# A gated mix of attention and a state-space filter: TensorE's queue per group of scores, and zero matmuls sized to a set activity

## The chip, the cores and the metric

The kernel runs on one core of one Trainium2 chip. The metric is the device time of one execution in microseconds (us), as the median of several runs. The engines are TensorE (PE in the profile, with its weight loads as PEld), VectorE (DVE), ScalarE (ACT), GpSimd (POOL) and SyncE (SP, whose queue issues nearly all DMAs). Each engine works through its own queue strictly in the order in which the program wrote it.

## The reference, cut to what matters

```python
x = A_x                                            # 1 x 2048 x 512, bf16
g = sigmoid((x * gate_w).sum(-1, keepdims=True))
# a: attention, 32 heads of 16 channels, no mask
q, k, v = split_heads(x @ wqkv)
a = merge_heads(softmax(q @ k.T * 16 ** -0.5) @ v) @ wo
# b: per channel d a convolution of x over time with a kernel of 128 complex modes
dt   = exp(log_dt)
K    = einsum("dn,dnl,dn->dl", C, exp(dt * A * l), dt * B).real
b    = causal_conv(x, K) + x * Dskip
out  = g * a + (1 - g) * b
```

The attention part has 32 heads of 2048 x 2048 scores, and each score goes through an exponential.

## The kernel before, in words

**Slots and groups.** The scores are cut into 2048 *slots* of 128 keys x 512 queries of one head. Four slots (four heads of one half of a 128-channel strip) make a *quad*, 16 quads a *block* (512 queries, all keys), 32 blocks the whole. Independently of quads, three slots in a row make a *group*: there are 683 groups. For group g, TensorE writes three score matmuls into a PSUM tile of three banks, `SC[g % 2]` (`qk`, line 662), ScalarE takes the exponential of all three at once, 128 x 1536, into a ring of 15 slots in SBUF, `ET` (`ex`, line 673, L675). The values are accumulated per quad by four matmuls into the PSUM bank `OA` (`pv`, line 678); each of them takes four slots, so there are three value quads in four groups. After the 16th quad of a block, VectorE transposes `OA` out (`norm_a`, L689), and the next block may use the bank.

**Background.** Everything else is cut into small segments, written as Python generators ("threads") that yield an engine, a cost and a priority: the projections of queries, keys and values (`projs`), the gate (`gate`), the parameters, bases and tables of the state-space part on VectorE (`params`, `base`, `table`), its convolution kernels (`kstage`, tile `Kst`), its chunk states (`sstage`: `Qt` x `X2` into the bank `MB`, evicted to `Sst` by VectorE, L986 and L988), a scan over 32 chunks on VectorE (`scan`, L1037 to L1053, tiles `G`, `s2`, `s3`), its outputs (`ystage`: `Tt` x `X2` and `Py` x `SG` into `MB`, evicted to `Yst`, L1118) and the output projection (`outs`, `Wo`). All of these share the one PSUM bank `MB`, taken with a lock.

**What sets the order.** The program is written out by a planner when it is built. The planner keeps a modelled clock for every engine (`p.tm`), adds a written-in cost for every instruction (`c=`), and a latency (`lat=`) before another engine may see its result. For each group it records the exponential, then the score matmuls of the next group, and then calls `fill`, which picks segments whose modelled start is early enough: a PE segment is taken if it would end by `pe_until`, 0.35 us after the modelled end of ScalarE's queue. A value quad is one of these segments, with a priority that excuses it from the test of its end.

**Zero matmuls.** After `fill`, the planner may add matmuls of a tile of zeros, `wm`, that accumulate zeros into `OA` and change nothing. Each instruction on PE has a count `a`, its columns weighted by the share of the 128 x 128 array that it uses: 512 for a matmul of 512 columns on the whole array, 128 for a score or a value matmul of 512 columns (a quarter of the rows, or of the columns). `p.act` sums these counts over a group.

```python
        sch.fill(t, t + .35)
        lack = min(lack, 1536) + FILL - p.act
        b = sch.now
        while lack > 256 and b is not None and p.tm["PE"] < t + .2:
            mm(OA ..., wm ..., wm ...)          # 512 columns
            lack -= 512
        p.act = 0
```

`FILL` is 1400. `lack` is carried from group to group; it is cut off above 1536 and not cut off below. `b` is the block whose accumulation is open in `OA`. All PE instructions are recorded through one helper, `mm`, so that they all stand under line L551 in the profile, and are told apart by their tiles: `SC<-Qm,KT` are scores, `OA<-ET,VE` values, `OA<-wm` zeros, `MB<-...` background. At the end of the build `place` lays the SBUF tiles out, tiles whose lifetimes do not meet on the same bytes, with waits for what lay there before.

Of the kernel before, what the change touches and what calls it, by code (L numbers as in the profile page):

```python
# [10 lines left out]
ALU = mybir.AluOpType  # L11

P = 128
S = 2048
D = 512
# [8 lines left out]
FILL = 1400  # L24
# [31 lines left out]
class Prog:  # L56
# [61 lines left out]
    def ready(self, a):  # L118
        eng, R, W = a[1][0], a[1][2], a[1][3]
        t = 0.0  # L120
        for acc, wr in ((R, False), (W, True)):
            for b, sl, *tag in acc:
                st = b.st.get(sl)
                if not wr and (st is None or not st[0] or (tag and b.tags.get(sl) != tag[0])):
                    return None
                if st is None:
                    continue
                for d in (st[0], st[1]) if wr else (st[0],):
                    for s, i in d.items():
                        if s != "PE" or eng != "PE":  # L130
                            t = max(t, self.fin[(s, i)] + (0 if s == eng else .08))
        return t
# [28 lines left out]
    def op(self, eng, fn, R=(), W=(), c=.1, lat=.05, a=0):  # L161
        if self.cap is not None:
            self.cap.append((self.op, (eng, fn, R, W), dict(c=c, lat=lat, a=a)))
            return
        self.act += a
        self.log.append((self.op, self.q, (eng, fn, R, W)))
        deps = self._deps(eng, R, W)
        i = self.cnt[eng]
        at = self.tm[eng]
        for s, k in deps.items():  # L170
            at = max(at, self.fin[(s, k)] + (0 if s == eng else .08))
        self.tm[eng] = at + c
        self.fin[(eng, i)] = at + c + lat
        self.cnt[eng] += 1
        self._record(eng, fn, deps, eng, i, R, W)
        return at + c + lat
# [58 lines left out]
class Sched:  # L235


    def __init__(self, prog):
        self.p = prog
        self.thr = []  # L240
        self.flag = set()
        self.lock = {}
        self.now = None
        self.n = 0

# [79 lines left out]
    def fill(self, until, pe_until):  # L325
        while True:
            best = None
            for t in self.thr:
                e = self.est(t)
                if e is None:  # L330
                    continue
                if t.eng == "PE":
                    if e + t.cost > pe_until and t.up > 0 or e > pe_until:
                        continue
                elif e > until:
                    continue
                now = self.p.tm[t.eng]
                k = (max(e, now + .3) if e > now + .02 else now, t.up, t.n)
                if best is None or k < best[0]:
                    best = (k, t)  # L340
            if best is None:
                return
            self.issue(best[1])
# [22 lines left out]
def declare(nc, es):  # L366
# [75 lines left out]
    sb("X2", 4 * 32 * 64)  # L442
# [19 lines left out]
def place(nc, bufs):  # L462
# [20 lines left out]
    for k in range(400):  # L483
# [7 lines left out]
        if best is None or top < best[0]:  # L491
            best = (top, order)
    assert best[0] <= end, (best[0] - end, live(sbs))
# [38 lines left out]
def dv(n, r=1):  # L532
    return .1 + n * 1.045e-3 / r


def record(nc, p, B, ins):
# [10 lines left out]
    MM, QUAD, TRI = .23, .34, .33  # L547
# [85 lines left out]
    def proj_ev(kind, idx, c, bank):  # L633
# [3 lines left out]
           [(o, ky)], c=.65)  # L637

    def vproj_mm(pi, kq, i, q4):
        kt = 4 * kq + i  # L640
        mm(lambda: MB(128 * i, [[1, 128]]), lambda: xT(q4 * S + 128 * kt, [[1, 128]]), lambda: B["Wv"](q4 * D + 128 * pi, [[1, 128]]),
           [xk(kq, q4), (B["Wv"], 0)], [(MB, 0, ('p', "V", pi, kq))], q4 == 0, q4 == 3, c=.08, a=128)

    def vproj_ev(pi, kq):
        op("DVE", lambda v: v.tensor_copy(VE((pi * 16 + 4 * kq) * VW, [[VW, 4], [17, 8], [1, 16]]),
                                          MB(0, [[128, 4], [16, 8], [1, 16]])),
           [(MB, 0, ('p', "V", pi, kq))], [(VE, (pi, 4 * kq + i)) for i in range(4)], c=.68)

    def mk_qm(b):
        qc, pi, w = b // 8, (b % 8) // 2, b % 2  # L650
        op("DVE", lambda v: v.tensor_scalar(Qm(512 * (b % 2), [[1, 512]]), B[f"Q{qc}"](512 * pi, [[1, 512]]),  # L651
                                            msk(w, [[1, 1]]), None, ALU.mult), [(B[f"Q{qc}"], pi), (msk, 0)], [(Qm, b % 2, b)], c=.32)
# [20 lines left out]
    def ex(g):  # L673
        sc, e, n = SC[g % 2], (3 * g) % NS, len(slots(g))
        op("ACT", lambda a: a.activation(ET(512 * e, [[1, 512 * n]]), sc(0, [[1, 512 * n]]), AF.Exp, scale=DH ** -0.5),  # L675
           [(sc, i, g) for i in range(n)], [(ET, s % NS, s) for s in slots(g)], c=.063 + .4267 * n, lat=.1)
# [11 lines left out]
    def norm_a(b):  # L688
        op("DVE", lambda v: v.transpose(OT(0, [[1, 512]]), OA(0, [[1, 512]])), [(OA, 0, b)], [(OT, 0, b)], c=.72)  # L689

    def norm_b(b):
# [3 lines left out]
                                            Rz(16 * w, [[1, 16], [0, 16]]), ALU.mult), [(OT, 0, b), (Rz, w)], [(ON, w)], c=.4)  # L695

    def norm_c(b):
        qc, pi = b // 8, (b % 8) // 2
        op("DVE", lambda v: v.transpose(OnT[qc](pi * 512, [[1, 512]]), ON(0, [[1, 512]])), [(ON, 0), (ON, 1)],
           [(OnT[qc], pi)], c=.7)  # L700
# [153 lines left out]
    def base(qr, eng):  # L854
# [4 lines left out]
        for l, n in ((0, "VV"), (1, "VL")):  # L859
            yield (eng, .38)  # L860
            op(eng, lambda v, l=l, n=n: v.tensor_copy(FP(l, [[e8, 2], [8, 128]]), B[n](d0, [[D, 2], [1, 128]])), key(n), [(FP, 0)], c=.38)
# [30 lines left out]
    def table():  # L892
# [3 lines left out]
        for pb in range(NBLK // 2):  # L896
# [9 lines left out]
            for i in range(2):  # L906
                yield ("DVE", .4)
                op("DVE", lambda v, i=i, b0=b0, B16=B16: v.tensor_copy(PT(i * PTN, [[CB * T, 2], [T, CB], [1, 16]]),
                                                                     B16(b0 + i * CB * 16, [[2048, 2], [16, CB], [1, 16]])), bk, [W[i]], c=.38)
# [21 lines left out]
    X2 = B["X2"]  # L931
# [37 lines left out]
    def sstage(blk):  # L969
        yield ("AFTER", f"ub{blk // 4}")  # L970
        q0, qr, bl = (blk % 2) * PTN, blk // 4, blk % 4
        for bank in range(4):
# [3 lines left out]
            for pp in range(2):  # L976
                yield ("PE", .29)
                for j in range(4):
                    k, par = 4 * bank + 2 * pp + j // 2, j % 2
                    mm(lambda pp=pp, j=j: MB(256 * pp, [[1, 256]], 32 * j, 32),  # L980
                       lambda k=k, par=par: X2(2048 * qr + 16 * bl + k, [[64, 32]], 64 * par, 64),
                       lambda k=k, par=par: Qt(q0 + 128 * k, [[16 * 128, 2], [1, 128]], 64 * par, 64),
                       [(Qt, (blk % 2, k // 8), blk), (Qt, (blk % 2, 2 + k // 8), blk), (X2, (qr, par))], [(MB, 0, ('S', blk, bank))], pos=(64 * par, 32 * j),
                       c=.29 if j == 0 else 0, a=32)
            yield ("DVE", .8, -1)
            op("DVE", lambda v, bank=bank: v.tensor_copy(Sst(512 * bank, [[256, 2], [1, 128]]), MB(0, [[256, 2], [1, 128]])),  # L986
               [(MB, 0, ('S', blk, bank))], [(Sst, bank, (blk, bank))], c=.37)
            op("DVE", lambda v, bank=bank: v.tensor_scalar(Sst(512 * bank + 128, [[256, 2], [1, 128]]), MB(128, [[256, 2], [1, 128]]),  # L988
                                                           -1.0, None, ALU.mult),
               [(MB, 0, ('S', blk, bank))], [(Sst, (bank, 1), (blk, bank))], c=.37)  # L990
# [32 lines left out]
    def scan():  # L1023
# [4 lines left out]
        def quarter(qr):  # L1028
# [4 lines left out]
            for c in range(NCH - 1):  # L1033
                so = 2 * SGH * (c + 1)
                if c == 0:
# [9 lines left out]
                yield (e, .38)  # L1045
                op(e, lambda v, so=so: v.tensor_tensor(s2(0, [[128, 2], [1, 128]]), s2(0, [[128, 2], [1, 128]]),  # L1046
                                                             sg(so, [[SGH, 2], [1, 128]]), ALU.add),
                   [(s2, 0)] + ks, [(s2, 0)], c=.38)
                yield (e, .38)
                op(e, lambda v: v.tensor_tensor(G(0, [[1, 256]]), s2(0, [[1, 256]]), s3(0, [[1, 256]]), ALU.add),  # L1050
                   [(s2, 0), (s3, 0)], [(G, 0)], c=.38)
# [38 lines left out]
    def ystage():  # L1090
        def unit(u):
# [8 lines left out]
            for q in range(4):  # L1100
                yield ("PE", .2)
                for j in range(4):
                    par, k = j % 2, 2 * q + j // 2
                    mm(lambda q=q, j=j: MB(64 * q, [[1, 64]], 32 * j, 32),
                       lambda k=k, par=par: X2(2048 * qr + 16 * bl + 8 * hf + k, [[64, 32]], 64 * par, 64),
                       lambda k=k, par=par: Tt(r * 512 + 64 * k, [[1, 64]], 64 * par, 64),
                       [(X2, (qr, par)), (Tt, (r, par, k // 4), u)], ky, True, False, pos=(64 * par, 32 * j), c=.2 if j == 0 else 0, a=8)
                yield ("PE", .35)
                for ri in range(2):
                    for j in range(4):  # L1110
# [5 lines left out]
                           pos=(0, 32 * j), c=.2 if j == 0 else 0, a=16)  # L1116
# [22 lines left out]
    def ublocks():  # L1139
        yield ("AFTER", "base1")  # L1140
        for qr in range(4):
            for par in range(2):
                yield ("SP", .5)
                dma("SP", lambda e, qr=qr, par=par: e.dma_start(X2(2048 * qr, [[64, 32], [1, 64]], 64 * par, 64),
                                                               B["xrd"].dram(64 * qr + 256 * par, [[32 * D, 64], [D, 32], [1, 64]])),
                    [(B["xrd"], 0)], [(X2, (qr, par))], c=.5, lat=5)
# [48 lines left out]
    def outs():  # L1195
# [3 lines left out]
        for lt in range(16):  # L1199
# [4 lines left out]
            for pi in range(3 if lt >= 12 else 4):  # L1204
# [6 lines left out]
               [(MB, 0, ('o', lt)), (Yl, ("c", lt))] + key("g"), W, c=.68)  # L1211
# [5 lines left out]
    def projs():  # L1217
# [5 lines left out]
        for kind, i, c in todo:  # L1223
            yield ("LOCK", "MB")
            for q4 in range(4):
                if kind == "V":
                    yield ("PE", .32)
# [71 lines left out]
    for q4 in range(4):  # L1299
        proj_mm("K", 0, 0, (SC[0], 0, 0), q4)  # L1300
    op("DVE", lambda v: v.tensor_scalar(Qm(0, [[1, 512]]), OA(0, [[1, 512]]), msk(0, [[1, 1]]), None, ALU.mult),
       [(OA, 0, ('p', "Q", 0, 0)), (msk, 0)], [(Qm, 0, 0)], c=.68)
# [23 lines left out]
    for g in range(NG):  # L1326
# [11 lines left out]
        sch.fill(t, t + .35)  # L1338
        lack = min(lack, 1536) + FILL - p.act
        b = sch.now  # L1340
        while lack > 256 and b is not None and p.tm["PE"] < t + .2:
            mm(lambda: OA(0, [[1, 512]]), lambda: wm(0, [[1, 128]]), lambda: wm(0, [[1, 512]]), [(wm, 0)], [(OA, 0, b)], False, False)
            lack -= 512
# [15 lines left out]
    for i in range(4):  # L1359
# [4 lines left out]
           [(b, sl, ('o', lt)), (fp, lt - 12)] + key("g"), [(fo, lt % 4, lt)], c=.68)  # L1364
# [35 lines left out]
```

## Time and profile before

| | |
|---|---|
| median of 3 runs | 1030.11 us (1026.2, 1030.11, 1030.48) |
| the profiled execution, span from first to last instruction | 1023.2 us |
| what the median has beyond that span | 6.9 us |
| ACT busy | 946.5 us (93%) |
| PE busy | 866.9 us (85%), 7076 matmuls |
| DVE busy | 611.4 us (60%) |
| mean clock granted to TensorE | 0.690 of full speed |
| exponentials | 683, 939.4 us busy together |
| zero matmuls in `OA` | 276 (nine of them before the first group), 123.5 us |

The profile gives no time of the profiled execution besides its span; what lies around the span is taken from the median. A busy PE in this profile is not a PE at its peak, since the ends of matmuls are modelled. The granted clock is listed in the profile as full or half speed over stretches of time; a mean such as 0.690 is a mix of these two. Durations of one instruction overlap with the next one's on the same engine, so that the pace is read from start to start or from busy time over count: an exponential of 128 x 1536 is listed as 1508 ns, and 109 of them in a row take 146.46 us, 1.344 us each.

The order of the background in time: projections until 152 us, tables and bases on VectorE, chunk states from 222 to 492 us, outputs of the state-space part from 460 to 708 us, output projection from 715 us on. From about 775 us to the last exponential at 1012.56 us there is little on TensorE besides scores, values and zeros.

### The profile page before, as it was taken

What the parts mean: (1) busy time and instruction counts of PE and PEld (TensorE: products, weight loads), DVE (VectorE), ACT (ScalarE), POOL (GpSimd) and SP (SyncE); (2) the same over time, 40 slices, a digit from 0 to 9 for tenths busy, and PEclk for the clock granted to TensorE, in tenths of its full rate; (3) what the DMA queues carried; (4) which work ended last, traced back from release to release, by engine and by line L of the source; (5) the groups of instructions that cost most, each with busy time, mean ns of one, the idle gap of its engine ahead of it and who ended that gap; (6) DMA issues with size and microseconds to landing.
All of it is one profiled execution on the core that took longest, in us unless ns stands there. A gap on an engine that the chain in (4) does not pass through costs nothing.

```text
span 1023.2 us, 17025 instructions
## 1 busy us (share of the span) xinstructions
PE 866.9 (85%) x7076; PEld 246.4 (24%) x7076; DVE 611.4 (60%) x1382; ACT 946.5 (93%) x693; POOL 11.9 (1%) x15
## 2 busy tenths in 40 slices
PE   7888788789889888889989899899887787787786
PEld 3332322112112222223323233233211111111111
DVE  4899999987678998878889988702310000000201
ACT  6999999999889999989999999999999899989985
POOL 4000000000000000000000000000000000000000
PEclk9999995555556887655565665755957766767757
DMA  8200005259997788696475725142100000000000
GB/s 180 83 2 1 2 1 83 103 119 202 232 240 176 170 186 208 187 176 165 108 145 145 168 75 148 40 124 48 42 11 11 1 1 1 1 1 1 1 1 21
DMA packets 228940, 92.21 MB, mean 90 GB/s; under 512 B 193408, under 2 KB 216576, under 8 KB 226816
## 3 DMA queue, kind: packets, MB, share of 16 engines
q1 hardware_dynamic: 227136, 90.22, 38.5%
q10 hardware_dynamic: 1728, 0.92, 0.4%
q8 instruction: 55, 0.90, 0.3%
q14 instruction: 21, 0.17, 0.0%
HBM read 27.92 MB, written 35.65 MB: 62 GB/s over the span
## 4 chain that ended last, share of the span: by engine, by line
ACT 51%; PE 41%; DVE 2%; SPq 2%; DMA 2%; issue 2%; ACTq 0%; DVEq 0%
ACT ET L675 51%; PE OA L551 19%; PE SC L551 14%; PE MB L551 9%; SPq L1017 1%; DMA Wq<-in_A_wqkv_dram 1%; DMA Qt<-gm_ptd 0%; SPq L937 0%; DVE Sst L986 0%; DMA Tt<-gm_kpd 0%; DVE Sst L988 0%; DVE OT L689 0%; DVE Kst L958 0%; SPq L994 0%; ACTq L555 0%
## 5 line engine op out<-in xcount | busy, mean ns | idle before, releaser
L675 ACT ACTIVATE ET<-SC 128x1536 bf16<-128x1536 f32 (+1 forms) x683 | 939.4, 1508 | 62.1 <-PE SC L551 55.7
L551 PE MATMUL OA<-ET,VE 128*32 128x512 bf16 x2048 | 268.6, 514 | 117.4 <-ACT ET L675 114.1
L551 PE MATMUL SC<-Qm,KT 32*128 32x512 bf16 x2048 | 353.2, 511 | 11.3 <-ACT ET L675 9.7
L551 PEld LDWEIGHTS SC<-Qm,KT 32*128 32x128 bf16 x2048 | 69.5, 95 | 275.9 <-issue 203.6
L551 PE MATMUL OA<-wm 128*128 128x512 bf16 x276 | 123.5, 573 | 1.2 <-DVE wm L604 1.2
L551 PEld LDWEIGHTS OA<-ET,VE 128*32 128x32 bf16 x2048 | 56.8, 100 | 268.9 <-ACT ET L675 242.0
L651 DVE TENSOR_SCALAR Qm<-Q,msk 128x512 bf16<-128x512 bf16 x31 | 10.6, 342 | 178.7 <-PE SC L551 178.7
L689 DVE STREAM_TRANSPOSE OT<-OA 128x512 f32<-128x512 f32 x32 | 22.9, 714 | 74.2 <-PE OA L551 74.1
L703 DVE TENSOR_TENSOR tt<-B,D 128x1024 bf16<-128x1024 bf16 x96 | 63.2, 683 | 0.3
L1050 DVE TENSOR_TENSOR G<-s,s 128x256 f32<-128x256 f32 x120 | 50.7, 422 | 3.4
L551 PE MATMUL MB<-Qt,X 64*32 64x256 bf16 x512 | 43.3, 392 | 8.8 <-issue 3.2
L1040 DVE TENSOR_TENSOR s<-G,MU 128x256 f32<-128x256 f32 x120 | 50.1, 417 | 0.1
L1046 DVE TENSOR_TENSOR s<-s,SG 128x256 f32<-128x256 f32 x120 | 50.1, 417 | 0.0
L1043 DVE TENSOR_TENSOR s<-G,MU 128x256 f32<-128x256 f32 x120 | 50.0, 417 | 0.0
L551 PE MATMUL MB<-Py,SG 128*32 128x64 bf16 x1024 | 44.1, 259 | 0.0
L1118 DVE CAST Yst<-MB 128x256 bf16<-128x256 f32 x32 | 13.5, 423 | 50.7 <-PE MB L551 50.5
L986 DVE CAST Sst<-MB 128x256 bf16<-128x256 f32 x64 | 27.0, 422 | 24.3 <-PE MB L551 23.8
L551 PEld LDWEIGHTS OA<-wm 128*128 128x128 bf16 x276 | 27.5, 119 | 57.4 <-issue 52.3
L1053 DVE CAST SG<-G 128x256 bf16<-128x256 f32 x120 | 34.9, 291 | 3.0
L551 PE MATMUL MB<-Tt,X 64*32 64x64 bf16 x512 | 35.7, 267 | 0.2 <-DMA Tt<-gm_kpd 0.2
L551 PEld LDWEIGHTS MB<-Py,SG 128*32 128x32 bf16 x1024 | 27.5, 150 | 34.9 <-issue 31.8
L703 DVE TENSOR_TENSOR ft<-FP,L 128x1024 f32<-128x1024 f32 (+1 forms) x32 | 33.8, 1079 | 0.0
(123 smaller groups left out, 470.2 us busy)
## 6 DMA issues: line engine op xcount, KB each, us to landing
gm_ptd<-PT SPq DMA_DIRECT2D x16, 1024.0 KB, 5.1
Py<-gm_ptd SPq DMA_DIRECT2D x32, 512.0 KB, 4.3
gm_sd<-Sst SPq DMA_DIRECT2D x64, 128.0 KB, 2.7
gm_kpd<-Kst SPq DMA_DIRECT2D x16, 256.0 KB, 4.3
Tt<-gm_kpd SPq DMA_DIRECT2D x128, 32.0 KB, 3.5
gm_xrd<-in_A_x_dram SPq DMA_DIRECT2D x1, 2048.0 KB, 12.1
X<-gm_xrd SPq DMA_DIRECT2D x8, 256.0 KB, 4.9
gm_ytd<-Yst SPq DMA_DIRECT2D x32, 64.0 KB, 4.0
```

The costliest lines, as they stand in the source:

```text
L551: op("PE", lambda t: t.matmul(out(), lhsT(), rhs(), start=start, stop=stop, skip_group_check=True, **kw), R, W, c=c, lat=.15, a=a)
L651: op("DVE", lambda v: v.tensor_scalar(Qm(512 * (b % 2), [[1, 512]]), B[f"Q{qc}"](512 * pi, [[1, 512]]), msk(w, [[1, 1]]), None, ALU.mult), ...
L675: op("ACT", lambda a: a.activation(ET(512 * e, [[1, 512 * n]]), sc(0, [[1, 512 * n]]), AF.Exp, scale=DH ** -0.5), [(sc, i, g) for i in ran ...
L689: op("DVE", lambda v: v.transpose(OT(0, [[1, 512]]), OA(0, [[1, 512]])), [(OA, 0, b)], [(OT, 0, b)], c=.72)
L703: op(eng, lambda v: v.tensor_tensor(o(), a(), b_(), f), R, W, c=c)
L986: op("DVE", lambda v, bank=bank: v.tensor_copy(Sst(512 * bank, [[256, 2], [1, 128]]), MB(0, [[256, 2], [1, 128]])), [(MB, 0, ('S', blk, ba ...
L1040: op(e, lambda v: v.tensor_tensor(s2(0, [[128, 2], [1, 128]]), G(0, [[128, 2], [1, 128]]), MU(d0, [[0, 2], [1, 128]]), ALU.mult), key("G", ...
L1043: op(e, lambda v: v.tensor_tensor(s3(0, [[128, 2], [1, 128]]), G(128, [[-128, 2], [1, 128]]), MU(D + d0, [[D, 2], [1, 128]]), ALU.mult), k ...
L1046: op(e, lambda v, so=so: v.tensor_tensor(s2(0, [[128, 2], [1, 128]]), s2(0, [[128, 2], [1, 128]]), sg(so, [[SGH, 2], [1, 128]]), ALU.add), ...
L1050: op(e, lambda v: v.tensor_tensor(G(0, [[1, 256]]), s2(0, [[1, 256]]), s3(0, [[1, 256]]), ALU.add), [(s2, 0), (s3, 0)], [(G, 0)], c=.38)
L1053: op(e, lambda v, so=so: v.tensor_copy(sg(so, [[SGH, 2], [1, 128]]), G(0, [[128, 2], [1, 128]])), key("G"), ks if c < NCH - 2 else [(sg, b ...
L1118: op("DVE", lambda v: v.tensor_copy(Yst(r2 * 256, [[1, 256]]), MB(0, [[1, 256]])), ky, [(Yst, r2, u)], c=.37)
```

## The change

It rewrites what the planner puts into TensorE's queue for each group, and the planner's costs.

1. **Order within a group.** A PE segment is no longer taken if its modelled start lies past the end of ScalarE's queue, value quads included. The value matmuls whose exponentials end with the present group are therefore written one group later; the order in the queue becomes scores of the next group, values that have ended, background, zeros.
2. **Size of the zeros.** The wanted count per group is `FILL`, now 1600, plus what the last group lacked, between -256 and 768. Background on PE is only taken if there is room left for the zeros that are still wanted (`room`). Zeros come in matmuls of 512 or of 256 columns, up to 0.3 us past ScalarE's modelled end. When `OA` is closed between two blocks, they go to `MB`, if no thread holds it.
3. **Pauses.** In the first 4 of every 14 groups the PE segments of threads with priority 2 or 5 (`sstage`, `ystage`, `gate`) are not taken, and the wanted count is at least 1792.
4. **The model's numbers.** Costs of VectorE and PE operations are written lower by a few hundredths of a microsecond, and the latencies between engines are changed.
5. **Tiles.** The tile `X2` becomes four tiles, and each quarter's two loads wait for its own `base` mark instead of all for `base1`. `place` tries up to 12,000 more layouts if the first 400 do not fit.

```diff
-FILL = 1400
+ZCOL = .213 / 512
+FILL = 1600
+OVER = .3
+REST = (14, 4, 1792)
+DLAG = .05
...
-                            t = max(t, self.fin[(s, i)] + (0 if s == eng else .08))
+                            t = max(t, self.fin[(s, i)] + (.03 if s == eng else DLAG if eng == 'PE' and s == 'DVE' else .05))
...
-    def op(self, eng, fn, R=(), W=(), c=.1, lat=.05, a=0):
+    def op(self, eng, fn, R=(), W=(), c=.1, lat=.085, a=0):
...
-    def fill(self, until, pe_until):
+    def fill(self, until, pe_until, want=0):
...
                 if t.eng == "PE":
-                    if e + t.cost > pe_until and t.up > 0 or e > pe_until:
+                    if self.rest and t.prio in (2, 5):
+                        continue
+                    own = sum(a[2].get("a", 0) for a in t.seg if isinstance(a, tuple))
+                    room = max(0, want - self.p.act - own) * ZCOL
+                    if e + t.cost + room > pe_until and t.up > 0 or e > min(until, pe_until):
                         continue
...
-    sb("X2", 4 * 32 * 64)
+    for k in range(4):
+        sb(f"X2{k}", 32 * 64)
...
+    k = 0
+    while best[0] > end and k < 12000:
...
 def dv(n, r=1):
-    return .1 + n * 1.045e-3 / r
+    return .07 + n / 960 / r
...
-    MM, QUAD, TRI = .23, .34, .33
+    MM, QUAD, TRI = .24, .33, .32
...
     def ublocks():
-        yield ("AFTER", "base1")
         for qr in range(4):
+            yield ("AFTER", f"base{min(qr + 1, 3)}")
...
         t = p.tm["ACT"]
-        sch.fill(t, t + .35)
-        lack = min(lack, 1536) + FILL - p.act
-        b = sch.now
-        while lack > 256 and b is not None and p.tm["PE"] < t + .2:
-            mm(lambda: OA(0, [[1, 512]]), lambda: wm(0, [[1, 128]]), lambda: wm(0, [[1, 512]]), [(wm, 0)], [(OA, 0, b)], False, False)
-            lack -= 512
+        want = FILL + min(max(lack, -256), 768)
+        sch.rest = g % REST[0] < REST[1]
+        if sch.rest:
+            want = max(want, REST[2])
+        sch.fill(t, t + OVER, want)
+        lack = want - p.act
+        p.act = 0
+        while lack >= 256 and p.tm["PE"] < t + OVER:
+            b = sch.now
+            if b is not None:
+                bank, W = OA, [(OA, 0, b)]
+            elif sch.lock.get("MB") is None:
+                bank, W = MB, [(MB, 0, "zero")]
+            else:
+                break
+            n = 512 if lack >= 512 else 256
+            mm(lambda bank=bank, n=n: bank(0, [[1, n]]), lambda: wm(0, [[1, 128]]), lambda n=n: wm(0, [[1, n]]), [(wm, 0)], W,
+               bank is MB, bank is MB, c=n * ZCOL, a=n)
+            lack -= n
         p.act = 0
```

The other edits of the diff are written-in costs of single operations (for example .65 to .62 for an eviction of 128 x 512, .29 to .22 for four matmuls of the chunk states).

## Prediction

> **What bounds the kernel now.** I read the page first: busy shares, the 40 slices, the costly groups.
>
> ```profile
> span 1023.2 us, 17025 instructions
> ...
> PE   7888788789889888889989899899887787787786
> ...
> ACT  6999999999889999989999999999999899989985
> ...
> PEclk9999995555556887655565665755957766767757
> ...
> L675 ACT ACTIVATE ET<-SC 128x1536 bf16<-128x1536 f32 (+1 forms) x683 | 939.4, 1508 | 62.1 <-PE SC L551 55.7
> ```
>
> ScalarE's 683 exponentials fill the span, and its idle time is spent waiting for scores. The clock row is full in the first six slices and a mix of full and half afterwards. Next, the chain that ended last, in order of time:
>
> ```profile
> 18.42 146.46 ACT ET L675 x109
> ...
> 809.76 1.82 PE OA L551 x4
> ```
>
> The first line is the pace when nothing disturbs it: 146.46 / 109 = 1.344 us a group. The second is typical of what interrupts it later: four matmuls into `OA` of 0.455 us each. Busy time and clock in stretches of 25 us (PE, PEld, DVE, ACT, POOL, then the clock):
>
> ```profile
> 125.00:150.00 25.00, 20.68 (x144) 5.41 (x142) 23.43 (x39) 25.00 (x20) 0.00 (x0) 1.00 0.00 1
> 175.00:200.00 25.00, 20.29 (x130) 3.80 (x126) 22.67 (x40) 24.51 (x19) 0.00 (x0) 0.50 0.38 124
> 600.00:625.00 25.00, 25.00 (x312) 9.21 (x308) 21.20 (x63) 23.48 (x18) 0.00 (x0) 0.50 0.52 128
> ```
>
> At full clock ACT is busy 25.00 of 25 us, and VectorE at 94% does not hurt it; at half clock ACT falls to 23.48. What sets the clock shows in two neighbouring stretches of 3.41 us, which is the length in which the trace lists it, first all engines, then zeros alone:
>
> ```profile
> 787.87:791.29 3.42, 1.91 (x21) 0.50 (x18) 1.40 (x3) 3.06 (x3) 0.00 (x0) 1.00 0.00 0
> 791.29:794.70 3.41, 3.41 (x18) 0.75 (x14) 0.00 (x0) 2.63 (x3) 0.00 (x0) 0.50 0.00 0
> ...
> 787.87:791.29 3.42, 0.00 (x0) 0.00 (x0) 0.00 (x0) 1.00 0.00 0
> 791.29:794.70 3.41, 1.89 (x4) 0.43 (x4) 0.00 (x0) 0.50 0.00 0
> ```
>
> Counted as the kernel counts (512 for a zero, 128 for a score or value matmul; weight loads do not straddle the edges), the first has 18 x 128 = 2304 and is followed by a half-clock stretch; the second has 10 x 128 + 4 x 512 = 3328 and is followed by a full one. I did this count for every 3.41-us stretch of the trace, spreading each matmul over its columns: above about 3000 the next stretch is full, below it half, with three exceptions in some 290. At 1.344 us a group a stretch holds 2.54 groups, so 1185 a group keeps the clock.
>
> Finally the durations, from TensorE's timeline around 803 us (full clock) and 809 us (half):
>
> ```profile
> 803.23 0.40 PE L551 MATMUL OA<-ET,VE 128*32 128x512 bf16 x4 [0.62 <-ACT ET L675]
> 803.56 0.39 PE L551 MATMUL SC<-Qm,KT 32*128 32x512 bf16 x3
> 803.89 1.04 PE L551 MATMUL OA<-wm 128*128 128x512 bf16 x4
> 804.86 0.39 PE L551 MATMUL SC<-Qm,KT 32*128 32x512 bf16 x3
> ...
> 808.60 0.62 PE L551 MATMUL OA<-ET,VE 128*32 128x512 bf16 x4 [0.62 <-ACT ET L675]
> 809.15 0.61 PE L551 MATMUL SC<-Qm,KT 32*128 32x512 bf16 x3
> 809.70 1.89 PE L551 MATMUL OA<-wm 128*128 128x512 bf16 x4
> 811.51 0.49 PE L551 MATMUL SC<-Qm,KT 32*128 32x512 bf16 x3
> ```
>
> From start to start: values 0.33 and 0.55, scores 0.33 and 0.55, four zeros 0.97 and 1.81. The zeros come four at a time in one group of four: only the group without a value quad passes the planner's test of PE's time. At half clock those 1.81 us delay the scores, and ACT idles 0.8 us.
>
> **The floor.** The first exponential starts at 14.54 us, the last at 1012.56 us; 682 steps of 1.344 are 916.4. So 1012.56 - 14.54 - 916.4 = 81.6 us is lost. Sorted by the clock at each step, 81.2 of it lies in the 401 groups at half clock (9.0 from 150 to 286 us, 13.9 to 450, 27.1 to 712, 31.2 to 1013), at full clock nothing. Without loss the span is 1023.2 - 81.6 = 941.6 us. Medians lie 6.9 us above the span; I add that.
>
> **The change, part by part.**
>
> *Zeros at 1600 a group, with the debt cut.* Ahead of the first group 33 matmuls count 512 each, 16,900; the 101 groups to 150 us count some 1664 each, 264 over `FILL`, which makes `lack` about -43,600. From 150 to 286 us the 94 groups count 913 each, so `lack` climbs by 487 a group, 45,800 together: no zero is written until 286 us, and the clock is 0.52 there. With the cut at -256 that goes. Scores and values count 768 a group, so 832 columns of zeros or background are added. At full clock a group takes PE 0.33 + 0.75 x 0.33 + 832 x 0.97 / 2048 = 0.97 us of 1.344: hidden behind ACT. 1600 x 2.54 = 4064 against 3000 keeps the clock. If that cover goes (half clock), the group takes 0.55 + 0.41 + 832 x 1.81 / 2048 = 1.70 us and costs 0.35 on the path, but counts 1600 x 3.41 / 1.70 = 3210 a stretch and so ends itself.
>
> *The same with background.* The bank `MB` keeps PE 110 us over the 286 groups from 286 to 712 us, 0.38 a group, worth some 130 in the count. At half clock: 0.55 + 0.41 + 0.38 + 702 x 1.81 / 2048 = 1.96 us, 0.62 lost a group, 1600 x 3.41 / 1.96 = 2780: below 3000, so this holds itself down. The pause is what ends it: 0.96 + 1024 x 1.81 / 2048 = 1.87 us and 1792 x 3.41 / 1.87 = 3270 a stretch; four such groups last 7.5 us, more than two stretches, so one lies whole inside. An episode is then some 5 groups at 0.62 and 3 of the pause at 0.52: 4.7 us.
>
> *What starts an episode.* After 25 us PE stalls for over 1 us, other than for ACT, three times before the tail: 2.52 us at 280.1 (chunk states wait for the load of `Qt`), 2.23 at 293.1 (the scan's first operation waits 4.95 us for `SG` on VectorE, an eviction stands behind it, `kstage` behind that), 1.25 at 447.0 (`Qt`). ACT loses 2.92, 2.47 and 1.25. The loads are unchanged, so I keep all three: 6.6 us. The two long ones leave too little in their stretch to keep the clock: 2 x 4.7 = 9.4 us.
>
> *Values one group later.* No instruction is added. The ring has 15 slots, five groups, and the exponential that reuses a slot comes four groups after the values now do: zero. If that cover went, ACT would wait one quad, 0.33 us.
>
> *Pauses.* They delay background by at most 14/10. From 222 to 712 us that is 196 us if PE set its pace; VectorE, busy 85% there, sets it. Even so the output projection, now from 715 us on, would end before the last group: zero.
>
> *Zeros into `MB`* wait for VectorE's last read of it, with the next scores behind them: at most 0.42 us (an eviction, row of `Sst`), once in each of 32 blocks, inside the 0.37 us that PE has free: zero, bound 13.
>
> *Cheaper VectorE in the model.* 1024 elements in bf16 (row of `tt`) go start to start in 0.60 us, 0.635 in the old model, 0.603 in the new. Taken at zero; background matmuls wait now 11.8 us for `Sst`, which I keep as the bound above, and as much below.
>
> *`X2` in four, other layout.* The same eight loads of 256 KB on SP's queue, 4.9 us each; the last two come later, past `base2` and `base3`, with `Qt` and `ptd` transfers behind them, and `sstage` needs the last only for its last quarter. Zero; a new wait from bytes shared otherwise is bounded by one stall like the one at 280 us, 2.5, to either side.
>
> Sum: 941.6 + 6.6 + 9.4 = 957.6 us of span, 964.5 of time. The bounds taken at zero (13, 12 and 2.5 upwards) stay for the range.
>
> **A rule against it.** From 784 to 822 us PE never idles more than 0.95 us between matmuls, and five of the eleven 3.41-us stretches are at half clock; from 600 to 625 us it is busy all 25 us at 0.50. The Trainium skill, TensorE: Matmul & The Clock Gate, "Why this matters for your kernels", asks for no idle gaps above about 3 us to keep the rate. By that rule zeros would fill no gap that matters and the third rival below would hold; the trace disagrees.
>
> **The rivals.**
>
> 1. *Half clock between pauses* in part of the state-space stretch: more stalls than three, each lifted only by the next pause. 60 more groups at 0.62 give 37 us: about 1002. For it: chunk states and outputs there run at 0.50 now. Against it: at full clock (327 to 341 us) chunk states cost nothing. 0.16.
> 2. *The pauses do not lift the clock*, because `OA` is closed or `MB` locked within them, or a kernel segment lies inside. Then the 330 groups from 222 to 708 us stay at half clock and the larger zeros sit on the path: 205 us, 941.6 + 6.6 + 205 + 6.9 = 1160. It turns slower than now from (81.6 - 6.6) / 0.62 = 121 such groups on. For it: 3270 is only 9% above the threshold; against: `OA` is closed in one group of 21. 0.09.
> 3. *The clock does not follow the count.* Then all 401 groups at half clock pay 0.35 to 0.62 instead of today's 0.20: 1090 to 1200. Against it: 290 stretches. 0.02.
> 4. *The zeros do not get written* where they are wanted, and the last 300 us stay as they are; state-space slows as the pauses do: 1030. 0.03.
>
> **How the numbers follow.** Forecast 0.70, with its own range 945 (no loss, 948.5, and a median 3 us nearer the span, as the fastest run's 1026.2 is) to 990 (five episodes more). Rival 1 lies between 990 and 1024. Range 945 to 1015: beyond it lie rivals 2, 3 and 4 and the top of 1, about 0.18. The three runs differ by 0.4%, so 0.5% is about what a measurement can tell from no change. Faster: 0.70 + 0.16 = 0.86; same 0.03; slower 0.11.
>
> **What would show it.** Clock above 0.9 in the mean, full from 150 to 286 us; ACT over 85% of the chain; ACT's idle time for scores under 20 us; zeros in every group, over 700 of them. Wrong: half clock in whole slices between 222 and 708 us, with PE near 100% there; or stalls of PE behind `MB<-wm` or `MB<-Qt`.

## The result and the profile after

The changed kernel takes 963.8 us (median of 4 runs, 961.22 to 974.63) against 1029.59 us: a ratio of 0.9398 with a 95% interval of 0.934 to 0.9455. The profiled execution has a span of 959.4 us and took 961.22 us. Every execution listed from here on took 1.8 us longer than its span.

The page of the changed kernel, the lines that answer to those shown of the kernel before (its lines stand 22 further down: L697 is the exponential, L573 the helper of all matmuls):

```profile
span 959.4 us, 18513 instructions
...
PE   7888888888787888889999999998889998888885
...
ACT  7999999999897899999999999999998999999996
...
PEclk9999999999898999999999999999997999999999
...
ACT 80%; PE 8%; DVE 7%; DMA 3%; SPq 2%; issue 1%; DVEq 0%
...
L697 ACT ACTIVATE ET<-SC 128x1536 bf16<-128x1536 f32 (+1 forms) x683 | 919.9, 1842 | 18.1 <-PE SC L573 17.9
...
L573 PE MATMUL OA<-wm 128*128 128x512 bf16 (+1 forms) x1004 | 280.7, 355 | 1.2 <-DVE wm L626 1.2
```

The clock row is full except in three slices, ScalarE makes up 80% of the chain that ended last (51% before), and its idle time for scores went from 55.7 to 17.9 us. There are 1004 zeros in `OA` where there were 276, and 28 more in `MB`. The same three stretches of 25 us as before (PE, PEld, DVE, ACT, POOL, clock):

```profile
125.00:150.00 25.00, 22.11 (x165) 6.25 (x162) 24.38 (x40) 25.00 (x20) 0.00 (x0) 1.00 0.00 1
175.00:200.00 25.00, 20.32 (x160) 5.50 (x156) 23.82 (x42) 25.00 (x21) 0.00 (x0) 1.00 0.40 127
600.00:625.00 25.00, 24.30 (x311) 10.30 (x311) 4.07 (x9) 25.00 (x20) 0.00 (x0) 1.00 0.37 94
```

The third is dense state-space output; PE is nearly as busy as before (24.30 of 25 us), but at full clock, and ScalarE no longer waits. The chain in order of time has the undisturbed pace in long pieces:

```profile
17.34 158.47 ACT ET L697 x118
...
320.71 94.15 ACT ET L697 x70
...
575.81 143.85 ACT ET L697 x107
...
732.80 216.39 ACT ET L697 x161
```

Counting losses as the prediction did (step from one exponential to the next, less 1.344 us, sorted by the clock at its start) gives for the profiled executions:

| | lost, us | groups at half clock | lost in them | lost at full clock |
|---|---|---|---|---|
| before | 81.6 | 401 | 81.1 | 0.5 |
| after | 18.5 | 14 | 9.6 | 8.8 |

Of the 18.5 us, 5.8 lie between 150 and 286 us, 8.8 up to 450 us, and 3.8 after 712 us; from 450 to 712 us nothing is lost.

### The profile page after: what moved, and what is told of

Same layout as the page of the kernel before. It is cut to its first block, busy times and chain, and to the rows that moved or that the text cites. A ratio compares the mean times of both kernels' runs of the same rounds, so it can differ in the third digit from the quotient of the medians.

```text
span 959.4 us, 18513 instructions
## 1 busy us (share of the span) xinstructions
PE 832.6 (87%) x7832; PEld 283.8 (30%) x7832; DVE 610.0 (64%) x1382; ACT 927.0 (97%) x693; POOL 11.9 (1%) x15
## 4 chain that ended last, share of the span: by engine, by line
ACT 80%; PE 8%; DVE 7%; DMA 3%; SPq 2%; issue 1%; DVEq 0%
ACT ET L697 80%; PE OA L573 4%; PE SC L573 2%; PE MB L573 2%; SPq L959 1%; DMA gm_ptd<-PT 1%; DVE tt L725 1%; DVE G L1072 1%; DVE s L1062 1%; DVE s L1068 1%; DVE s L1065 1%; DVE SG L1075 1%; DVE PT L725 0%; DMA Qt<-gm_ptd 0%; DVE Sst L1008 0%
## 5 line engine op out<-in xcount | busy, mean ns | idle before, releaser
L697 ACT ACTIVATE ET<-SC 128x1536 bf16<-128x1536 f32 (+1 forms) x683 | 919.9, 1842 | 18.1 <-PE SC L573 17.9
L573 PE MATMUL SC<-Qm,KT 32*128 32x512 bf16 x2048 | 270.3, 389 | 90.7 <-ACT ET L697 83.7
L573 PE MATMUL OA<-wm 128*128 128x512 bf16 (+1 forms) x1004 | 280.7, 355 | 1.2 <-DVE wm L626 1.2
L573 PE MATMUL OA<-ET,VE 128*32 128x512 bf16 x2048 | 207.6, 396 | 4.0 <-DVE OT L711 3.5
L573 PEld LDWEIGHTS SC<-Qm,KT 32*128 32x128 bf16 x2048 | 66.4, 91 | 324.2 <-ACT ET L697 295.6
L573 PEld LDWEIGHTS OA<-wm 128*128 128x128 bf16 x1004 | 70.0, 98 | 106.6 <-issue 86.4
L573 PEld LDWEIGHTS OA<-ET,VE 128*32 128x32 bf16 x2048 | 52.8, 93 | 123.1 <-issue 113.6
L1140 DVE CAST Yst<-MB 128x256 bf16<-128x256 f32 x32 | 13.5, 422 | 99.1 <-PE MB L573 99.0
L673 DVE TENSOR_SCALAR Qm<-Q,msk 128x512 bf16<-128x512 bf16 x31 | 10.7, 346 | 64.6 <-PE SC L573 64.5
L573 PE MATMUL MB<-Qt,X 64*32 64x256 bf16 x512 | 31.6, 309 | 11.4 <-DVE Sst L1010 9.6
L1008 DVE CAST Sst<-MB 128x256 bf16<-128x256 f32 x64 | 26.8, 418 | 22.7 <-PE MB L573 22.0
L573 PE MATMUL MB<-Py,SG 128*32 128x64 bf16 x1024 | 38.5, 227 | 0.0
L573 PEld LDWEIGHTS MB<-Py,SG 128*32 128x32 bf16 x1024 | 31.7, 146 | 11.2 <-issue 5.7
L573 PE MATMUL MB<-Tt,X 64*32 64x64 bf16 x512 | 33.2, 247 | 2.0 <-DVE Sst L1010 0.9
```

The lines of the kernel that those rows point to most:

```text
L573: op("PE", lambda t: t.matmul(out(), lhsT(), rhs(), start=start, stop=stop, skip_group_check=True, **kw), R, W, c=c, lat=.15, a=a)
L1140: op("DVE", lambda v: v.tensor_copy(Yst(r2 * 256, [[1, 256]]), MB(0, [[1, 256]])), ky, [(Yst, r2, u)], c=.37)
```

## The experiments

Ratios are to the kernel before, timed on the same chip; the table gives the profiled execution's losses, counted as above. One profiled execution can lie some us off the median of its kernel: those of e3, e5, e6, e8, e9 and e11 are the slowest of their runs, that of e4 and the changed kernel's the fastest. The traces of e5 to e12 lack part of the zeros' records (e5's has 270 of 343), so that their TensorE busy times are too low; their exponentials are complete.

| | median, us | ratio, 95% interval | clock | lost | groups at half clock | lost in them / at full clock |
|---|---|---|---|---|---|---|
| e1 zeros on 32 rows | 1111.9 | 1.0807 (1.0775 to 1.0839) | 0.594 | 169.7 | 536 | 168.6 / 1.1 |
| e2 no zeros | 1000.3 | 0.9728 (0.9696 to 0.976) | 0.608 | 59.8 | 531 | 55.9 / 3.9 |
| e3 no pauses | 976.4 | 0.9489 (0.9459 to 0.952) | 0.955 | 37.1 | 35 | 20.7 / 16.4 |
| e4 DMA latencies | 954.1 | 0.928 (0.9233 to 0.9328) | 0.985 | 9.5 | 11 | 4.3 / 5.3 |
| e5 before + debt cut | 1034.3 | 1.0052 (1.0024 to 1.0079) | 0.699 | 97.3 | 379 | 98.4 / -1.1 |
| e6 before + order | 1014.4 | 0.9836 (0.9782 to 0.989) | 0.787 | 78.6 | 258 | 76.0 / 2.7 |
| e7 before + both | 977.7 to 1008.8 | none | 0.900 | 50.0 | 102 | 42.1 / 7.9 |
| e8 e4 + issue costs | 957.1 | 0.9308 (0.928 to 0.9336) | 0.978 | 17.5 | 17 | 8.2 / 9.3 |
| e9 FILL 1400 | 981.3 | 0.9513 (0.947 to 0.9555) | 0.941 | 40.5 | 52 | 24.7 / 15.8 |
| e10 FILL 1100 | 1012.3 | 0.9819 (0.9783 to 0.9855) | 0.617 | 69.4 | 515 | 64.7 / 4.7 |
| e11 no room | 979.4 | 0.9498 (0.9456 to 0.954) | 0.958 | 38.7 | 30 | 18.1 / 20.5 |
| e12 e4 + block ends | 950.5 | 0.9212 (0.9173 to 0.9251) | 0.983 | 7.5 | 10 | 4.6 / 2.9 |

**What sets the clock: e1.** The changed kernel, with each zero reading 32 rows instead of 128.

```diff
-mm(... lambda: wm(0, [[1, 128]]), lambda n=n: wm(0, [[1, n]]), ..., c=n * ZCOL, a=n)
+mm(... lambda: wm(0, [[1, 128]], 0, 32), lambda n=n: wm(0, [[1, n]], 0, 32), ..., pos=(0, 0), c=n * ZCOL, a=n)
```

> Every zero matmul reads 32 rows of the zero tile instead of 128: as many instructions, as many columns, as much time on TensorE, but a quarter of the count (columns times share of the array). It leaves nothing out. Theory A, the count sets the clock: 768 + 832 / 4 = 976 a group, 2480 in a stretch of 3.41 us, under the 3000 read off the trace of before; in a pause 1024 a group, 2600. So full clock to about 150 us (projections) and half clock after it, mean 0.55 to 0.65. The zeros then cost 0.35 us a group without background and 0.62 with it: 280 x 0.35 + 300 x 0.6 = 278 us on 941 plus 2, about 1220; since 32 rows of zeros can overlap scores of other rows, 1080 to 1220. Theory B, TensorE's busy time (or columns whatever their rows) sets the clock: mean 0.97 as in the changed kernel, 955 to 975 us.

It took 1111.9 us at a clock of 0.594: theory A's range and clock, though well under the 1220 us that its sum gave. Busy times from 450 to 712 us, of the changed kernel and of e1 (PE, PEld, DVE, ACT, POOL, clock):

```profile
450.00:712.00 262.00, 238.82 (x2638) 90.69 (x2636) 169.45 (x484) 261.86 (x196) 0.68 (x2) 1.00 0.46 102
```

```profile
450.00:712.00 262.00, 260.99 (x2323) 78.05 (x2319) 144.06 (x410) 215.46 (x151) 0.68 (x2) 0.50 0.48 102
```

In e1 TensorE is busy 260.99 of 262 us, more than in the changed kernel, and is at half clock all the time. The number of instructions and columns is the same; only the share of the array differs. So neither busy time nor columns alone hold the clock, and the count weighted by the share does. The count of the prediction, made over all 3.41-us stretches of e1's trace, agrees: with a quarter for the zeros, 2 of 323 stretches are on the wrong side of 3000, with the weight of a full matmul 208 are. The Trainium skill (TensorE: Matmul & The Clock Gate, "Why this matters for your kernels") asks for no idle gaps above about 3 us between matmuls; the longest wait of TensorE in this stretch is 0.6 us, and the clock stays at half.

**What half clock alone costs: e2.** The changed kernel with `FILL = -100000` and no pauses, so that no zeros are written after the warm-up.

> The changed kernel with no zeros after the warm-up and no pauses; order and costs of the rest as in the changed kernel. It leaves nothing out. Theory A (the clock alone loses the time): half clock from 150 us on as in the kernel before, no gain over its 1029 us, or at most 10 us. Theory B (a good part of the loss before was the four zeros in a row in front of late scores at half clock, 0.8 us each): without them a group takes 0.96 us of 1.344 at half clock, 1.34 with background, so the last 250 us lose next to nothing; with 0.10 a group from 150 to 286 us and 0.2 in some 300 groups of state-space work 941 + 2 + 9 + 60 = 1012, range 980 to 1015. Mean clock 0.57 to 0.65 by both.

1000.3 us, theory B: at a lower clock than the kernel before (0.608 against 0.690 in the profiled executions) it is 2.7% faster. The last stretch, of before and of e2:

```profile
712.00:1013.00 301.00, 241.47 (x1419) 56.53 (x1416) 34.33 (x71) 275.74 (x203) 0.00 (x0) 0.72 0.02 6
```

```profile
712.00:988.00 276.00, 210.35 (x1255) 40.83 (x1252) 25.04 (x49) 274.09 (x205) 0.00 (x0) 0.55 0.01 4
```

About as many exponentials (203 and 205) fit into 276 us instead of 301 although the clock is lower. In their old order, the zeros cost more there than the clock they bought, 30.3 us lost against 2.1. So the gain of 65.8 us has two parts: e2 reaches 29 of it without zeros, with the new order and costs, and the other 37 come with the zeros and the full clock. The kernel before without its zeros was not run, so how the 29 divide between the zeros and the rest of the change is not shown.

**The size: e9 and e10.** The changed kernel with `FILL` 1400 (pauses as they are), and with `FILL` 1100 and no larger size in the pauses.

```diff
-FILL = 1600
+FILL = 1400          # e9;  e10: 1100 and REST = (14, 4, 0)
```

> The changed kernel with FILL 1400 instead of 1600; pauses still want 1792. Theory A (the threshold near 3000 a stretch, 1185 a group, is what matters, and 1400 clears it): 3560 a stretch at ScalarE's pace, clock over 0.93, but the smaller margin lets more stalls and block ends drop the clock: 960 to 980 us. Theory B (the step from 1400 to 1600 carries much of what e7 lacks): 980 to 1005 us.

> The changed kernel with FILL 1100, and 1100 wanted in the pauses too, so below the 1185 a group worked out from the trace of before: 2790 a stretch at ScalarE's pace. Theory A: half clock from the end of the projections on, wherever no projection or output matmul adds to the count, mean clock 0.55 to 0.7; a group takes 0.96 + 332 x 0.00088 = 1.25 us of PE at half clock, so little is lost without background and 0.2 to 0.3 with it: 985 to 1020 us. Theory B (no sharp threshold; any regular activity holds the clock): clock over 0.85, 955 to 975 us.

e10 lies as theory A has it: 1012.3 us, clock 0.617, 515 groups at half clock, so a regular 1100 a group does not hold it. e9 holds it mostly, and its clock (0.941) is theory A's, but its 981.3 us lie just past theory A's upper end and within theory B's range: 52 groups at half clock instead of 14, and 15.8 instead of 8.8 us lost at full clock. Both clocks agree with the prediction's threshold of 1185 a group; what theory A had too low is what the step from 1400 to 1600 is worth. The part at full clock is stalls, in a queue of another order, and how much of the 17.5 us is margin and how much is this, one run does not separate.

**The parts alone, in the kernel before: e5, e6, e7.**

```diff
-        lack = min(lack, 1536) + FILL - p.act
+        lack = min(max(lack, -256), 1536) + FILL - p.act                              # e5, e7
...
-                    if e + t.cost > pe_until and t.up > 0 or e > pe_until:
+                    if e + t.cost > pe_until and t.up > 0 or e > min(until, pe_until):  # e6, e7
```

> The kernel before with one edit: the carried lack is cut off at -256 below. The queue then holds 334 zeros after the warm-up instead of 267, and the first of them comes with the first groups. Theory A (the four in a row are the harm): the stretch 150 to 286 us becomes like 712 to 1013 us of the kernel before, four zeros in every fourth group, clock 0.6 to 0.75 there and 0.15 us lost a group instead of 0.10: 1025 to 1040 us. Theory B (the debt was the main fault): full clock from 150 to 286 us, 9 us less: 1010 to 1022.

> The kernel before with one edit: a PE segment is not taken when its modelled start lies past the end of ScalarE's queue, so that values are written one group later. FILL stays 1400, the debt stays, there is no room kept for zeros and no pause. 437 zeros after the warm-up, because now every group passes the test of PE's time. Theory A (even spread of the zeros is the main part): 1400 x 2.54 = 3560 a stretch keeps the clock wherever there is little background, so the 30 us lost after 712 us and some of the 42 us from 286 to 712 us go; the 9 us up to 286 us stay: 965 to 995 us, clock 0.75 to 0.9. Theory B (1400 is too little or the room for zeros is what counts): 1000 to 1030 us.

> The kernel before with the two edits of e5 and e6 together: 557 zeros after the warm-up. Theory A: full clock nearly everywhere, what is left are stalls and half-clock episodes in the state-space stretch that no pause ends: 955 to 980 us, clock 0.85 to 0.97. Theory B (room, size 1600 and pauses carry the gain): 985 to 1015 us.

The debt cut alone brings nothing: the kernel is 0.5% slower, with an interval just above 1. From 150 to 286 us there are now zeros, four in a row, the clock goes from 0.52 to 0.72, and the loss from 8.9 to 14.2 us, as theory A has it. (In all, the trace loses 15.7 us more than that of before, while the medians differ by 6: it is the slowest of ten runs, 1041.2 us.) The order alone came out at 1014.4 us, in theory B's range. After 712 us it does what theory A wanted (30.3 us lost become 10.7), but from 450 to 712 us the loss rises from 26.9 to 45.0, in a profiled execution of 1020.7 us, 6 above the median. Both together give, in the execution of 992.9 us, the full clock after 712 us (nothing lost there), while 450 to 712 us still loses 23.7 at a mean clock of 0.81:

```profile
450.00:712.00 262.00, 231.50 (x2767) 91.75 (x2806) 190.48 (x551) 242.41 (x178) 0.68 (x2) 0.81 0.55 122
712.00:980.00 268.00, 198.50 (x1436) 55.14 (x1461) 32.83 (x66) 267.56 (x201) 0.00 (x0) 0.99 0.02 7
```

The four runs of e7 lie between 977.7 and 1008.8 us, in step with their clocks (0.936 down to 0.866), and spread too far for a ratio: one lies in theory A's range, three in theory B's, so neither is shown. That 1400 without room sits so near the threshold that each execution falls under it at other places is a guess; only one of the four has a trace.

**Room and pauses: e11 and e3.** The changed kernel with `room = 0`, and with `REST = (14, 0, 0)`.

> The changed kernel without the reservation: background is taken as soon as it would end by the limit, whatever zeros are still wanted. The zeros are nearly as many (995 instead of 1004 after the warm-up, by the program). Theory A (size, spread and pauses carry the gain, since background is seldom dense enough to push zeros out): 958 to 975 us. Theory B (the room is what keeps the clock in the state-space stretch, as e7 without it has 57 groups at half clock from 450 to 712 us): 980 to 1005 us.

> The changed kernel without the pauses (no group leaves out the state-space segments, none wants 1792). Theory A, as predicted: three or so episodes of half clock between 250 and 330 us start from stalls of TensorE and are ended by a pause; without it each lasts while background is dense, some 10 to 20 groups more at 0.62: 970 to 1000 us, clock 0.85 to 0.95. Theory B: the zeros end an episode by themselves in a lull of background and the pauses do nothing: 958 to 968 us, clock over 0.96.

Without room 979.4 us, just above theory A's range and just below B's; without pauses 976.4 us, theory A by the time, while the clock, 0.955, lies just above theory A's range and below theory B's. By the medians the pauses are worth some 13 us and the room some 16; the intervals of both ratios lie just above the changed kernel's. The pauses' share is not from 450 to 712 us, where e3 loses only 0.4: it lies from 150 to 450 us, where e3 loses 36.3 and the changed kernel 14.6. In both the half-clock groups (35 and 30 instead of 14) explain about half of the difference of the profiled executions, 11.1 of 18.6 and 8.5 of 20.2 us; the rest is longer stalls at full clock, probably since background is written at other places.

**What starts an episode: e4, e8, e12.** After 25 us the changed kernel has three waits of TensorE above 1 us before the tail. The first, on TensorE's and then on VectorE's timeline:

```profile
254.28 0.40 PE L573 MATMUL OA<-ET,VE 128*32 128x512 bf16 x4
258.11 0.44 PE L573 MATMUL MB<-Qt,X 64*32 64x256 bf16 x8 [3.42 <-DVE Sst L1010]
```

```profile
253.88 0.43 DVE L930 COPY PT<-B 128x1024 bf16<-128x1024 bf16 x1 [1.70 <-DMA gm_ptd<-PT]
256.36 0.43 DVE L930 COPY PT<-B 128x1024 bf16<-128x1024 bf16 x1 [2.05 <-DMA gm_ptd<-PT]
256.70 0.68 DVE L725 TENSOR_TENSOR tt<-B,D 128x1024 bf16<-128x1024 bf16 x1
257.30 0.42 DVE L1008 CAST Sst<-MB 128x256 bf16<-128x256 f32 x1
257.64 0.41 DVE L1010 TENSOR_SCALAR Sst<-MB 128x256 bf16<-128x256 f32 x1
```

VectorE waits in its queue until the old `PT` has been stored; the eviction of `MB` (L1008 and L1010) stands behind it, the next chunk-state matmul waits for that eviction, and the scores stand behind this matmul. The planner gives that store 5 us, the page has a median of 6.0. In e4 the planner's latencies are raised:

```diff
-    ... [(PT, i, blk)], [(ptd, blk)], c=.5, lat=5)
+    ... [(PT, i, blk)], [(ptd, blk)], c=.5, lat=8)
...          # load of Qt: lat 3 to 5, load of SG: 3 to 6, store of Sst: 2.5 to 4
```

> The changed kernel with the planner's latencies of four transfers raised, to what the trace shows under load: the store of PT 5 to 8, the load of Qt 3 to 5, the load of SG 3 to 6, the store of Sst 2.5 to 4 us. Theory A: of the 18 us of ScalarE's waits, those at 255, 292, 296 and 315 us and the half-clock groups behind them come from VectorE (or TensorE) waiting in its queue for such a transfer with an eviction of the bank MB behind it; written later, they go: span 944 to 953, time 946 to 956, waits of ScalarE for scores under 8 us. Theory B: DMA is saturated in that stretch, the waits only move: 958 to 970 us, waits of 15 us or more.

954.1 us (four runs from 950.7 to 961.7; the profiled one is the fastest), in theory A's range, with a ratio whose interval lies just below the changed kernel's; ScalarE waits 8.3 us for scores, just above the 8 expected. The waits at 255 to 320 us are shorter (2.06 us lost from 250 to 275 us instead of 5.13, nothing from 275 to 350 us instead of 7.8). One new wait of 3.9 us for `Tt` appears at 425 us and makes up most of what is left. e8 raises the modelled cost of issuing these transfers, too.

> e4 with the planner's issue costs on SP's queue raised as well, to what the trace shows (0.6 us instead of 0.4 to 0.5 for Tt, Py, Sst, Kst, Yst, PT), and the latencies of Tt to 4.5, Py to 5, Kst to 5, Yst to 4 us. Theory A: the one long wait left in e4, 3.9 us of TensorE for Tt at 425 us with the half-clock groups behind it (7 us), was a load written later into SP's queue than the planner thought; it goes: 944 to 953 us, waits of ScalarE for scores under 5 us. Theory B: the order shifts and another transfer is late instead: 950 to 960 us.

957.1 us: theory B. The wait for `Tt` is gone, and another transfer is late, a load of `Qt` at 411 us (5.9 us lost in one step):

```profile
416.24 0.66 PE L573 MATMUL MB<-Qt,X 64*32 64x256 bf16 x8 [5.42 <-DMA Qt<-gm_ptd]
```

The intervals of e4 and e8 overlap, so that e8 is worse than e4 is not shown.

The changed kernel's last episode of half clock starts without such a wait. TensorE around 718 us:

```profile
717.35 0.40 PE L573 MATMUL OA<-ET,VE 128*32 128x512 bf16 x4
717.57 0.27 PE L573 MATMUL MB<-Py,SG 128*32 128x64 bf16 x8
717.77 0.26 PE L573 MATMUL MB<-Tt,X 64*32 64x64 bf16 x4
718.37 0.39 PE L573 MATMUL SC<-Qm,KT 32*128 32x512 bf16 x3 [0.34 <-ACT ET L697]
718.69 0.33 PE L573 MATMUL MB<-Py,SG 128*32 128x64 bf16 x8
719.71 0.61 PE L573 MATMUL SC<-Qm,KT 32*128 32x512 bf16 x3 [0.69 <-ACT ET L697]
720.25 0.62 PE L573 MATMUL OA<-ET,VE 128*32 128x512 bf16 x4
```

A block ends with the values at 717.35 us; `OA` is closed until VectorE has read it, and the output stage holds `MB`. So for two groups there are no values and no zeros, the count is about 2750 from 716.0 to 719.4 us, under the threshold, and four stretches at half clock follow. e12 is e4 with one more edit: a new lock of `MB` is not taken by segments of priority 2 or more in the last four quads of a block.

```diff
+                    if self.kt >= 12 and t.prio >= 2 and any(c[0] == "LOCK" for c in t.conds):
+                        continue
```

> e4 with one more edit: a segment of priority 2 or more does not take the lock of MB in the last four quads of a block, so that at the block's end, when OA is closed, the zeros can go into MB. Theory A: the episode at 719 us of the changed kernel (four stretches at half clock, 4 us; again at 717 us in e8) starts where a block ends while MB is locked and two groups get neither values nor zeros; it can't happen any more: 945 to 953 us, clock 0.98 or more, and no half clock after 450 us. Theory B: fewer places for the state-space work push its transfers closer together and new stalls cost as much: 953 to 965 us.

950.5 us, the fastest of all, 0.9212 of the kernel before; its interval (0.9173 to 0.9251) lies below the changed kernel's (0.934 to 0.9455). No group after 450 us is at half clock. But e4's trace has none after 712 us either (e8's has seven, from 718 us on), and against e4 the intervals overlap: that this last edit helps is not shown, and the cause of the episode at 719 us is read from the lines above, not tested. The stretch from 450 us on in e12:

```profile
450.00:712.00 262.00, 230.34 (x2547) 89.91 (x2589) 161.66 (x462) 262.00 (x196) 0.68 (x2) 1.00 0.46 100
712.00:938.00 226.00, 191.53 (x1830) 67.24 (x1862) 50.25 (x118) 226.00 (x170) 0.00 (x0) 1.00 0.15 38
```

ScalarE is busy throughout: from there to the end nothing is left but the exponentials' own pace.

## Why the prediction was right, step by step

**The floor** held: 13.5 us to the first exponential, 916.4 us of pace and 11.1 after the last start are 940.9 us, where 941.6 was predicted.

**The rule for the clock** held, in the unit in which it was stated. It was an inference from one trace; e1 (a quarter of the rows) and e10 against e9 (1100 and 1400 a group) show it.

**Stalls and episodes** held in sum, in part by luck: 6.6 and 9.4 us were predicted, 8.8 us at full clock and 9.6 at half clock were measured. The episodes behind stalls lost 5.2 us instead of 9.4, and one that was not foreseen added 4.4. The places were only partly right. The stall by `Qt` at 280 us did not come back as such; two of the three now start with VectorE waiting for a store and running late, and the episode at 719 us comes, as read above, from a block end, which the prediction had put at one group in 21 and given no price.

**The pauses** are worth time, as predicted, but not only in the way that was predicted. That "the pause is what ends" an episode fits the last one, which runs into a pause and through it (719.4 to 733.1 us); those of 258.6, 296.2 and 316.7 us hold one group of a pause or none. In its favour, e3, without pauses, has two long ones, of 9 groups (from 324 us) and of 11 groups (from 431 us). By e3's trace about half of what the pauses bring is fewer or shorter stalls, which the prediction did not have.

**The price of a half-clock group** with background, 0.62 us, held where the zeros use the whole array: the seven groups of the episode at 719 us lose 4.4 us, 0.63 each, and the 25 of e3 from 286 to 450 us lose 15.3, 0.61 each (short stalls within them included). e1, at half clock throughout, loses only 60.0 us over 151 groups from 450 to 712 us, 0.40 each, and takes 1112 us where rival 2 has 1160. But it is not rival 2's case, since its zeros of 32 rows run beside the scores:

```profile
601.75 0.60 PE L573 MATMUL OA<-wm 32*128 32x512 bf16 x1
601.75 1.02 PE L573 MATMUL SC<-Qm,KT 32*128 32x512 bf16 x3
```

Of the 183 zeros of 512 columns in that stretch, 136 have a score matmul start within 0.05 us of them, while four zeros on the whole array take 1.81 us at half clock before the next matmul starts. What rival 2 would have cost, no run shows.

**The debt cut** was described as a gain by itself. Alone it is none (e5, 0.5% slower); with the new order it probably is (e7 against e6: losses of 50.0 against 78.6 us, in one trace of each). The prediction named the four in a row as the harm but did not give the spread a price of its own; after 712 us, where there was little besides scores, values and zeros, 30.3 us were lost with the old zeros and 2.1 in e2 without any.

**What lies around the span** was wrong: 6.9 us were added, where 1.8 is right. The rest of the 6.9 was that the profiled execution of before was a fast one. The predicted span, 957.6 us, answers to a span of 959.4; that the predicted 964.5 us is so near the median of 963.8 is luck in this term: the profiled execution of after, too, is faster than its median, by 2.6 us.

**Small readings** that change no sum: VectorE's wait for `SG` before 292.1 us is 4.2 us in the trace, not 4.95, and from 222 to 708 us there are 325 groups, not 330. Of the signs that were named, ScalarE's share of the chain is 80% and not over 85%, and 142 of the 683 groups have no zeros, over half of them before 150 us, where the projections add to the count.

The rivals: 2 and 3 did not happen, and e1 excludes 3; 4 did not happen, zeros are in all stretches; 1 did not happen either, and e3, e9 and e11 come nearest to it, with 16 to 38 more groups at half clock and 976 to 981 us.

## What to carry to other kernels

When a clock gate goes by the work that an engine does, find its count and threshold in the trace of before, and then give each small time unit its share of filler: evenly, after the work that others wait for, and bounded on both sides, since the same filler in bursts at the low clock can cost more than the clock is worth. Leave margin above the threshold and look for the places where filler can't be written (a closed accumulator, a locked bank). Then what is left are waits in an in-order queue, and the planner's latencies for loaded transfers are the next thing to measure.

## What the runs showed of the hardware that was not expected

The step in the count lies near 3000 a stretch and depends on rows: 32-row matmuls of 512 columns count a quarter (e1), and such matmuls can run beside score matmuls. A kernel can have TensorE busy 99.6% of 262 us and stay at half clock. And half clock by itself costs this kernel little where TensorE has room: e2 loses 2.1 us in the 203 groups after 712 us, 184 of them at half clock.
